# Linear attention, then an MLP: k and v loaded with nine tokens a partition and two heads side by side

## The chip, the cores and the metric

The kernel runs on one core of a Trainium2 chip. The metric is the time of one execution on the device in microseconds (us), less being better. The time before is the median of three runs. A profiled execution stands beside them; its span runs from the first to the last instruction. Engine names are those of the profile: PE is the matrix engine (PEld its weight loads), DVE the vector engine, ACT the scalar engine, POOL the general one, SP the queue that issues most transfers. PSUM is the memory that PE writes its sums into[...]; SBUF is the working memory of 128 partitions.

## The reference

There are 8 batches, 8 heads, 576 tokens (S) and 64 channels a head (D). The attention is linear, with cosine weights on the position; its output is the input x of a mixer with a low-rank token mix and a two-layer MLP.

```python
theta = np.pi / 2.0 * pos / S
phi(x) = concatenate([relu(x) * cos(theta), relu(x) * sin(theta)], axis=-1)   # 64 -> 128 features
q_p, k_p = phi(q), phi(k)
kv = einsum('bhsf,bhsd->bhfd', k_p, v)
z = sum(k_p, axis=2)
x = einsum('bhsf,bhfd->bhsd', q_p, kv) / (einsum('bhsf,bhf->bhs', q_p, z)[..., None] + 1e-6)
x -> [8, 576, 512]                       # heads side by side
u = x + (x^T @ U @ V)^T                  # U: 576x32, V: 32x576
out = u + relu(u @ w_ch1) @ w_ch2        # w_ch1: 512x2048, w_ch2: 2048x512
```

k's contraction runs over tokens. Which token lies on which partition, and in which order tokens are added, therefore does not matter for kv, as long as k and v agree; q's tokens decide where the rows of x stand.

## The kernel before, in words

**Layout.** A batch's 576 tokens are split into 512 and a tail of 64. Of the 512, partition p has tokens 4p to 4p+3, so each transfer (`load_main`, L75) has runs of four tokens, 1024 bytes, for each head and partition. The tail (`load_tail`, L81) has one token a partition on 64 partitions, runs of 256 bytes; even batches use partitions 0 to 63, odd ones 64 to 127 (`tail`). The staging tiles are `qst`, `kst`, `vst` for the main part and `qt`, `kt`, `vt` for the tail.

**Scaling.** `k_prep` and `q_prep` handle one chunk c at a time (0 to 3 are the four tokens of a partition, 4 is the tail): one instruction for the cosine half and one for the sine half, each on DVE (L230) or ACT (L228), over 8 heads x 64 channels. `cosw` and `sinw` hold the weight of each partition's token in a column for each chunk. The tail chunk goes into `k_tl` or `q_tl`, whose other 64 partitions were set to zero at the start. v is cast to `v_ext` (`v_prep`, `v_block`), with a column of ones after each head's 64, so that z comes out as column 65 of kv.

**kv.** `kv_unit` (L262) makes four heads: for each head five matmuls of 128 features x 65 columns, contracting 128 tokens each, accumulate in a PSUM tile; then one instruction casts the tile into `kv`. A batch takes two calls, 40 matmuls.

**After kv.** q is transposed, by PE (`qtr_unit`) for batches 0 to 2 and by DMA for the others. `x_unit` makes x for batches 2 to 7; for batches 0 and 1 the quicker chain `den_unit` (denominators, `rec`) and `xh_unit` does it. `A_unit` makes x^T U in 32-column tiles of PE, `u_unit` adds the low-rank part, and `g1_main`, `g1_tail` (g_ps, L491 and L511) and `g2_part` (o_ps, L543) are the two MLP layers, with ACT evicting `hid` (L500).

**Order.** The order of every engine's instructions is that of the program text. The main part is a list of slots, each one step of an MLP layer (four 512-column matmuls as a rule), for four pairs of batches. Between the slots, `PLAN` puts the attention of batches 2 to 7: for each batch a slot w at which kv is made, offsets for v, k, q and the loads, and the engines for each. Batches 0 and 1 are ordered by hand: batch 0's scalings and `chain0` come ahead of all slots, and batch 1's stand in `beside` and `chain1`, beside the first slots of batch 0. `keep_warm` issues matmuls on zeros, so that PE is not idle. PSUM tags stand for buffers: "X" two banks, "T" one, "g" three of one bank, "o" two of one bank.

**Loads at the start.** SP issues in the order: q half, q half, k half, k tail, q tail, v half's tail, v half, k half, v half's tail, v half (a half is four heads). A POOL instruction, `mark` (L738), reads a cell of batch 0's first v half; behind it in POOL's order stands the first load of w_ch1 (`w1_load`, L91), which therefore starts only when that half of v has landed.

Of the kernel before, what the change touches and what calls it, by code (L numbers as in the profile page):

```python
# [10 lines left out]
FP32 = mybir.dt.float32  # L11
# [6 lines left out]
def kernel(  # L18
# [28 lines left out]


    def tail(b):
        lo = TS * (b % 2)  # L50
        return slice(lo, lo + TS)
# [7 lines left out]

    kst, vst, qst, kt, vt, qt = {}, {}, {}, {}, {}, {}  # L60

    def alloc_k(b):
        kst[b] = pool.tile([P, H, 4, D], FP32, tag="kst", bufs=2, name="kst")
        kt[b] = pool.tile([P, H, D], FP32, tag="kt", bufs=2, name="kt")

    def alloc_v(b):
        vst[b] = pool.tile([P, H, 4, D], FP32, tag="vst", bufs=1, name="vst")
        vt[b] = pool.tile([P, H, D], FP32, tag="vt", bufs=1, name="vt")

# [41 lines left out]
    alloc_v(0)  # L111
    iota = const.tile([P, 5], FP32)
    nc.gpsimd.iota(
# [3 lines left out]
    for lo in (0, TS):  # L117
        nc.gpsimd.iota(
            out=iota[lo : lo + TS, 4:5], pattern=[[1, 1]], base=512, channel_multiplier=1,
            allow_small_or_imprecise_dtypes=True,  # L120
        )
    load_main(qst[0], q, 0, 0, 4)
    load_main(qst[0], q, 0, 4, 8)
    load_main(kst[0], k, 0, 0, 4)
    load_tail(kt[0], k, 0)
    load_tail(qt[0], q, 0)
    load_tail(vt[0], v, 0, 0, 4)
    load_main(vst[0], v, 0, 0, 4)
    load_main(kst[0], k, 0, 4, 8)
    load_tail(vt[0], v, 0, 4, 8)  # L130
    load_main(vst[0], v, 0, 4, 8)
    zero = const.tile([P, 512], BF16)
    V_.memset(zero, 0.0)
    halfpi = const.tile([P, 1], FP32)
    nc.vector.memset(halfpi, math.pi / 2.0)
    cosw = const.tile([P, 5], FP32)
    sinw = const.tile([P, 5], FP32)
    scale_ang = math.pi / (2.0 * S)
# [6 lines left out]

    k_tl = const.tile([P, H, 2 * D], BF16)
    v_ext = [const.tile([P, 5, H, E], BF16, name=f"v_ext{i}") for i in range(2)]
    q_tl = const.tile([P, H, 2 * D], BF16)
# [14 lines left out]
    for i in range(2):  # L163
        nc.gpsimd.dma_start(out=U_bf[tail(i), 4 + i, :], in_=moe_U[512:S, :])
    for g in range(4):
        V_.tensor_copy(out=four[:, g, :], in_=ident[0:R, 0:R])
    for i in range(2):
        V_.memset(v_ext[i][:, 4, :, :], 0.0)
        V_.memset(v_ext[i][:, 0:4, :, D:E], 1.0)
        V_.memset(v_ext[i][tail(i), 4, :, D:E], 1.0)  # L170
    V_.memset(k_tl, 0.0)
    V_.memset(q_tl, 0.0)
    V_.memset(q_tlT, 0.0)
    V_.memset(x_tl, 0.0)

    def keep_warm(n, tag, bufs):
# [30 lines left out]

    def v_prep(b, h0=0, h1=H, cs=range(5), engs=None):
        vx = v_ext[b % 2]
        for n, c in enumerate(cs):  # L210
            eng = engs[n] if engs else G_
            if eng is None:
                continue
            if c < 4:
                cast(eng, vx[:, c, h0:h1, 0:D], vst[b][:, h0:h1, c, :])
            else:
                cast(eng, vx[tail(b), 4, h0:h1, 0:D], vt[b][tail(b), h0:h1, :])

    def v_block(b, h0, h1, c0, c1, eng):
        cast(  # L220
            eng,
            v_ext[b % 2][:, c0:c1, h0:h1, 0:D].rearrange("p c h d -> p h c d"),
            vst[b][:, h0:h1, c0:c1, :],
        )

# [7 lines left out]

    def prep(dst, src, b, c, engs, h0, h1):
        rows = slice(0, P) if c < 4 else tail(b)
        for i, (w, eng) in enumerate(zip((cosw, sinw), engs)):
            if eng is not None:
                scaled_relu(
                    eng, dst[rows, h0:h1, i * D : i * D + D], src[rows], w[rows, c : c + 1]
                )  # L240

    def k_prep(b, c, engs, h0=0, h1=H):
        if b not in k_p:
            k_p[b] = pool.tile([P, 4, H, 2 * D], BF16, tag="k_p", bufs=1, name="k_p")
        src = kst[b][:, h0:h1, c, :] if c < 4 else kt[b][:, h0:h1, :]
        prep(k_p[b][:, c] if c < 4 else k_tl, src, b, c, engs, h0, h1)

    def q_prep(b, c, engs, h0=0, h1=H):
        if b not in q_p:
            q_p[b] = pool.tile([P, 4, H, 2 * D], BF16, tag="q_p", bufs=1, name="q_p")  # L250
        src = qst[b][:, h0:h1, c, :] if c < 4 else qt[b][:, h0:h1, :]
        prep(q_p[b][:, c] if c < 4 else q_tl, src, b, c, engs, h0, h1)

    def kv_unit(b, hg, tag, bufs, eng=None):
        if b not in kv_sb:
            kv_sb[b] = pool.tile([P, H, E], BF16, tag="kv", bufs=2, name="kv")
        acc = ps.tile([P, 4, E], FP32, tag=tag, bufs=bufs, name="kv_ps")
        vx = v_ext[b % 2]
        for i in range(4):
            h = hg * 4 + i  # L260
            for c in range(5):
                nc.tensor.matmul(  # L262
                    out=acc[:, i, :],
                    lhsT=k_p[b][:, c, h, :] if c < 4 else k_tl[:, h, :],
                    rhs=vx[:, c, h, :],
                    start=(c == 0),
                    stop=(c == 4),
                )
        cast(eng or V_, kv_sb[b][:, hg * 4 : hg * 4 + 4, :], acc)

# [298 lines left out]
    def loads(b, eng):  # L569
        def kk():  # L570
            alloc_k(b)
            load_tail(kt[b], k, b, eng=eng)
            load_main(kst[b], k, b, eng=eng)

        def vv():
            alloc_v(b)
            load_tail(vt[b], v, b, eng=eng)
            load_main(vst[b], v, b, eng=eng)

        def qq():  # L580
            alloc_q(b)
            load_tail(qt[b], q, b, eng=eng)
            load_main(qst[b], q, b, eng=eng)

        return kk, vv, qq
# [20 lines left out]
    def attention_plan(b):  # L606
# [4 lines left out]
        def put(at, f, *a, tag=False):  # L611
            if tag:
                a = a + spare(w + at)
            plan.append((w + at, lambda: f(b, *a)))

        for n, c in enumerate(ORD):
            put(v_at[0] + v_at[1] * n, v_prep, 0, H, (c,), (v_at[2],))
        for n, c in enumerate(ORD):
            put(k_at[0] + n, k_prep, c, VA if b == 3 and n > 1 else k_at[1])
            e0, e1 = q_at[1]  # L620
# [4 lines left out]
        if qtr is not None:  # L625
            for n, (c0, c1) in enumerate(((0, 2), (2, 4), (4, 5))):
                put(qtr + 2 * n, qtr_dma, c0, c1)
        put(0, kv_unit, 0, tag=True)
        put(2, kv_unit, 1, tag=True)
        for n, c in enumerate(ORD if qtr is None else range(5)):  # L630
# [25 lines left out]

    def chain0():
        v_prep(0, 0, 4, (4,), (A_,))
        v_block(0, 0, 4, 0, 3, V_)
        v_block(0, 0, 4, 3, 4, A_)  # L660
        qtr_unit(0, 4, 0, H, V_, *G3)
        keep_warm(2, "o", 2)
        for c in (0, 1):
            k_prep(0, c, (V_, A_), 4, 8)
        kv_unit(0, 0, "T", 1)
        keep_warm(2, "o", 2)
        for c in (2, 3):
            k_prep(0, c, (V_, A_), 4, 8)
        k_prep(0, 4, (A_, A_), 4, 8)
        rec0 = den_unit(0, 0, 4, "X", 1)  # L670
        v_prep(0, 4, 8, (4,), (G_,))
        v_block(0, 4, 8, 0, 4, G_)
        w1_load(1)
        for n, c in enumerate(TL):
            xh_unit(0, c, 0, 4, rec0, *(O2, O2, G3, G3, G3)[n], A_ if n == 1 else None)
        keep_warm(1, "X", 1)
        kv_unit(0, 1, "T", 1, A_)
        rec1 = den_unit(0, 4, 8, "X", 1)
# [13 lines left out]
    def chain1(fill):  # L692
        kv_unit(1, 0, "T", 1)
        fill(0)
        rec0 = den_unit(1, 0, 4, "X", 1)
        v_block(1, 4, 8, 0, 4, A_)
        fill(1)
        for n, c in enumerate(ORD):
            xh_unit(1, c, 0, 4, rec0, *O2)
            if n == 1:  # L700
                fill(2)
            if n == 3:
                kv_unit(1, 1, "T", 1, A_)
        fill(3)
# [27 lines left out]
    V_evac(V_)  # L732
    for c in TL:
        k_prep(0, c, (V_, A_ if c < 3 else V_), 0, 4)
    q_prep(0, 4, (V_, A_))
    keep_warm(10, "o", 2)

# [3 lines left out]
    alloc_q(1)  # L741
    load_main(qst[1], q, 1)
    load_tail(qt[1], q, 1)
    alloc_k(1)
    load_main(kst[1], k, 1)
    load_tail(kt[1], k, 1)
    alloc_v(1)
    load_tail(vt[1], v, 1)
    load_main(vst[1], v, 1, 0, 4)
    load_main(vst[1], v, 1, 4, 8)  # L750
    chain_end(0, a0)
# [14 lines left out]
    for n, c in enumerate(ORD):  # L766
# [3 lines left out]
        at(1 + n, lambda c=c, tg=tg: qtr_unit(1, c, eng=V_, tag=tg[0], bufs=tg[1]))  # L770
        at((4, 5, 5, 6, 6)[n], lambda c=c, n=n: k_prep(1, c, (V_, A_)))
    at(2, lambda: G_.tensor_copy(out=mark, in_=q_tlT[0:TS, 0, TS : TS + 1]))
    at(2, lambda: [w1_load(2), w1_load(3)])
    at(2, lambda: v_prep(1, 0, H, (4,), (G_,)))
    at(2, lambda: v_block(1, 0, 4, 0, 4, G_))
    at(6, lambda: [w2_load(n) for n in range(4)])
# [70 lines left out]
```

## Time and profile before

| | us |
|---|---|
| median of 3 runs (319.23 to 320.55) | 320.3 |
| profiled execution, its own time | 319.13 |
| its span | 317.4 |
| PE busy | 307.9 |
| DVE busy | 156.5 |
| ACT busy | 150.8 |
| POOL busy | 36.4 |

The engines' busy times overlap each other, so they don't add up to the span. PE's share is an average: PE is busy 19.15 of the first 24 us, part of that on zeros, 22.52 of the next 24, and nearly all the time after that. The granted clock of PE was full throughout. The loads of k and v are 1024 KB and 128 KB for a batch each: in the table of transfers `kst` takes a median of 7.9 us from issue to landing and `kt` 6.1.

### The profile page before, as it was taken

What the parts mean: (1) busy time and instruction counts of PE and PEld (TensorE: products, weight loads), DVE (VectorE), ACT (ScalarE), POOL (GpSimd) and SP (SyncE); (2) the same over time, 40 slices, a digit from 0 to 9 for tenths busy, and PEclk for the clock granted to TensorE, in tenths of its full rate; (3) what the DMA queues carried; (4) which work ended last, traced back from release to release, by engine and by line L of the source; (5) the groups of instructions that cost most, each with busy time, mean ns of one, the idle gap of its engine ahead of it and who ended that gap; (6) DMA issues with size and microseconds to landing.
All of it is one profiled execution on the core that took longest, in us unless ns stands there. A gap on an engine that the chain in (4) does not pass through costs nothing.

```text
span 317.4 us, 5790 instructions
## 1 busy us (share of the span) xinstructions
PE 307.9 (97%) x2378; PEld 161.6 (51%) x2378; DVE 156.5 (49%) x355; ACT 150.8 (48%) x260; POOL 36.4 (11%) x67
## 2 busy tenths in 40 slices
PE   6889899999999999999999999999999999999996
PEld 2566554475545444475455444574454444464443
DVE  7879653843877554037826584254736510001211
ACT  5749655686806256659300187559300166650000
POOL 4324301200121220000121100000121100000000
PEclk9999999999999999999999999999999999999999
DMA  7999999964386928860999569900691130001122
GB/s 225 314 267 269 205 232 331 323 185 168 94 189 166 300 67 188 253 206 2 206 256 294 192 131 232 327 9 33 158 191 68 66 83 0 2 0 68 66 89 77
DMA packets 83803, 51.82 MB, mean 163 GB/s; under 512 B 52066, under 2 KB 81026, under 8 KB 83778
## 3 DMA queue, kind: packets, MB, share of 16 engines
q1 hardware_dynamic: 76850, 40.05, 47.3%
q0 software_dynamic: 6784, 11.35, 15.0%
q8 instruction: 18, 0.29, 0.4%
q10 hardware_dynamic: 144, 0.07, 0.1%
q14 instruction: 7, 0.06, 0.1%
HBM read 36.86 MB, written 9.44 MB: 146 GB/s over the span
## 4 chain that ended last, share of the span: by engine, by line
PE 87%; DMA 5%; ACT 4%; SPq 1%; DVE 1%; POOL 0%; issue 0%; DVEq 0%
PE o_ps L543 39%; PE g_ps L491 33%; PE gt_ps L511 4%; DMA w_bf<-in_moe_w_ch_dram 3%; PE kv_ps L262 3%; PE va_ps L407 3%; PE x_ps L363 3%; DMA vst<-in_v_dram 2%; ACT hid L500 2%; PE a_ps L390 1%; PE t_ps L279 1%; ACT k_p L228 1%; ACT q_p L228 1%; SPq L81 1%; SPq L75 0%; POOL mark L738 0%
## 5 line engine op out<-in xcount | busy, mean ns | idle before, releaser
L500 ACT ACTIVATE hid<-g_ps 128x512 bf16<-128x512 f32 x128 | 76.2, 596 | 100.8 <-PE g_ps L491 100.4
L543 PE MATMUL o_ps<-w_bf,hid 128*128 128x512 bf16 (+2 forms) x528 | 119.2, 373 | 0.0
L491 PE MATMUL g_ps<-uT,w_bf 128*128 128x512 bf16 x512 | 118.5, 379 | 0.1
L491 PEld LDWEIGHTS <-w_bf 128*128 128x128 bf16 x512 | 48.8, 98 | 56.0 <-issue 0.4
L543 PEld LDWEIGHTS <-hid 128*128 128x128 bf16 x528 | 48.7, 98 | 52.8 <-issue 1.7
L553 DVE TENSOR_TENSOR o_sb<-u_bf,o_ps 128x512 f32<-128x512 bf16 (+2 forms) x33 | 22.1, 668 | 62.7 <-PE o_ps L543 62.6
L563 POOL DMA_DIRECT2D out_dram<-o_sb x24 | 13.5, 561 | 165.0 <-DVE o_sb L553 155.0
L408 DVE TENSOR_TENSOR u_bf<-x_bf,va_ps 128x512 bf16<-128x512 bf16 x32 | 21.7, 685 | 10.2 <-PE va_ps L407 10.1
L105 DVE CAST kv<-kv_ps 128x260 bf16<-128x260 f32 x14 | 6.0, 428 | 31.6 <-PE kv_ps L262 31.6
L373 DVE TENSOR_TENSOR x_bf<-x_ps,rec 128x512 bf16<-128x512 f32 x24 | 16.6, 691 | 0.8
L228 ACT ACTIVATE q_p<-qst,sinw 128x512 bf16<-128x512 f32 (+1 forms) x24 | 15.1, 658 | 2.2 <-DMA qst<-in_q_dram 2.2
L511 PE MATMUL gt_ps<-uT_tl,w_bf 128*128 128x128 bf16 x256 | 15.6, 219 | 0.0
L407 PE MATMUL va_ps<-A_sb,V_bf 128*128 128x512 bf16 x40 | 15.2, 379 | 0.0
L543 PE MATMUL o_ps<-w_bf,hid_tl 128*128 128x512 bf16 x64 | 15.1, 379 | 0.0
L230 DVE TENSOR_SCALAR k_p<-kst,cosw 128x512 bf16<-128x512 f32 (+1 forms) x31 | 14.9, 503 | 0.0
L313 DVE TENSOR_SCALAR rec<-x_ps 128x8 f32<-128x8 f32 (+1 forms) x30 | 4.9, 165 | 20.2 <-PE x_ps L363 20.2
L511 PEld LDWEIGHTS <-w_bf 128*128 128x128 bf16 x256 | 14.6, 98 | 0.5
L262 PEld LDWEIGHTS <-k_p 128*128 128x128 bf16 x256 | 11.4, 97 | 4.8 <-ACT k_p L228 1.2
L262 PE MATMUL kv_ps<-v_ext,k_p 128*128 128x65 bf16 x256 | 12.2, 193 | 0.9 <-ACT k_p L228 0.9
L518 ACT ACTIVATE hid_tl<-gt_ps 128x512 bf16<-128x512 f32 x16 | 9.4, 597 | 5.5 <-PE gt_ps L511 5.5
L363 PEld LDWEIGHTS <-q_pT 128*128 128x128 bf16 x192 | 9.1, 98 | 5.5 <-issue 0.6
L230 DVE TENSOR_SCALAR q_p<-qst,cosw 128x512 bf16<-128x512 f32 (+1 forms) x28 | 11.6, 435 | 0.1
(106 smaller groups left out, 253.1 us busy)
## 6 DMA issues: line engine op xcount, KB each, us to landing
qst<-in_q_dram SPq DMA_DIRECT2D x7, 1024.0 KB, 8.9
kst<-in_k_dram SPq DMA_DIRECT2D x7, 1024.0 KB, 7.9
vst<-in_v_dram SPq DMA_DIRECT2D x6, 1024.0 KB, 8.2
out_dram<-o_sb POOLq DMA_DIRECT2D x24, 256.0 KB, 3.6
w_bf<-in_moe_w_ch_dram POOLq DMA_DIRECT2D x8, 512.0 KB, 9.3
vst<-in_v_dram SPq DMA_DIRECT2D x4, 512.0 KB, 7.9
out_dram<-o_sb SPq DMA_DIRECT2D x7, 256.0 KB, 2.4
qst<-in_q_dram SPq DMA_DIRECT2D x2, 512.0 KB, 3.8
```

The source lines that it names most:

```text
L228: nc.scalar.activation(out=o, in_=i, func=AF.Relu, bias=0.0, scale=w)
L230: eng.tensor_scalar(out=o, in0=i, scalar1=0.0, scalar2=w, op0=ALU.max, op1=ALU.mult)
L262: nc.tensor.matmul(out=acc[:, i, :], lhsT=k_p[b][:, c, h, :] if c < 4 else k_tl[:, h, :], rhs=vx[:, c, h, :], start=(c == 0), stop=(c == 4),)
L363: nc.tensor.matmul(out=acc[:, g, i * E : i * E + E], lhsT=qT_of(b, c, h), rhs=kv_sb[b][:, h, :], start=True, stop=True,)
L373: nc.vector.tensor_tensor(out=x_of(b, c, rows).rearrange("p (g i d) -> p g i d", g=2, d=D), in0=view[:, :, :, 0:D], in1=rec[rows].unsqueez ...
L407: nc.tensor.matmul(out=va, lhsT=V_bf[:, c, :], rhs=A_sb[b], start=True, stop=True)
L408: nc.vector.tensor_tensor(out=u_bf[b][:, c, :] if c < 4 else u_tl[b // 2][rows, :], in0=x_of(b, c, rows), in1=va[rows, :], op=ALU.add,)
L491: nc.tensor.matmul(out=g_ps.rearrange("p (c t) -> p c t", c=4), lhsT=w1_bf[:, d, j * P : j * P + P], rhs=uT[b][:, :, d, :], start=(d == 0) ...
L500: nc.scalar.activation(out=hid[b][:, j, :], in_=g_ps, func=AF.Relu, bias=0.0, scale=1.0)
L511: nc.tensor.matmul(out=g_ps[:, jj, :], lhsT=w1_bf[:, d, j * P : j * P + P], rhs=uT_tl[pr][:, d, :], start=(d == 0), stop=(d == 3),)
L543: nc.tensor.matmul(out=o[:, cols], lhsT=lhs[:, j, c * P : c * P + P], rhs=w2_bf[:, j, cols], start=(j == 0), stop=(j == NJ - 1),)
L553: nc.vector.tensor_tensor(out=o_sb[:, cols], in0=u[:, cols], in1=o[:, cols], op=ALU.add)
```

## The change

k and v of a batch are laid out anew. Partition p of the lower half (0 to 63) has tokens 9p to 9p+8 of the even head of a pair, and partition 64+p the same tokens of the odd head. All 576 tokens fit, so k and v have no tail; a run is nine tokens, 2304 bytes, and one transfer (`load_nine`) brings all four head pairs, or two of them. q stays as it was.

- `k_prep` has nine chunks instead of five, each of 4 pairs x 64 = 256 elements on 128 partitions instead of 512. The weights for them are columns 5 to 13 of `cosw` and `sinw`.
- `v_prep` casts one head pair at a time (9 x 64 elements), four instructions a batch; `v_block` is gone.
- `kv_unit` contracts 64 tokens a matmul: for each pair and chunk one matmul on the lower 64 partitions into one PSUM bank and one on the upper 64 into another, 72 a batch instead of 40. Batches 2 to 7 make it in one call with one cast at w+1; batches 0 and 1 in two calls. The tile has the tag X of two banks.
- `k_tl` and the zeroing of v's tails are gone; the `four` copies come after the other settings of constants.
- Batch 0's loads go q half, q half, k half, v half, q tail, k half, v half, and its scalings and `chain0` are ordered anew, with POOL taking part of k's second half. `den_unit` of the first half takes T instead of X. Batch 1's k comes before its q tail, and its scalings run three chunks a slot in slots 4 to 6.

```diff
+    def load_nine(dst, src, b, g0=0, g1=4, eng=None):
+        (eng or nc.sync).dma_start(
+            out=dst[:, g0:g1, :, :].rearrange("p g c d -> p g (c d)"),
+            in_=src[b].rearrange("(g hh) (p c) d -> (hh p) g (c d)", hh=2, c=9)[:, g0:g1, :],
+        )
...
-    load_main(kst[0], k, 0, 0, 4)
-    load_tail(kt[0], k, 0)
+    load_nine(kst[0], k, 0, 0, 2)
+    load_nine(vst[0], v, 0, 0, 2)
     load_tail(qt[0], q, 0)
-    load_tail(vt[0], v, 0, 0, 4)
-    load_main(vst[0], v, 0, 0, 4)
-    load_main(kst[0], k, 0, 4, 8)
-    load_tail(vt[0], v, 0, 4, 8)
-    load_main(vst[0], v, 0, 4, 8)
+    load_nine(kst[0], k, 0, 2, 4)
+    load_nine(vst[0], v, 0, 2, 4)
...
     for i in range(2):
-        V_.memset(v_ext[i][:, 4, :, :], 0.0)
-        V_.memset(v_ext[i][:, 0:4, :, D:E], 1.0)
-        V_.memset(v_ext[i][tail(i), 4, :, D:E], 1.0)
-    V_.memset(k_tl, 0.0)
+        V_.memset(v_ext[i][:, :, :, D:E], 1.0)
...
+    def v_prep(b, g, eng):
+        cast(eng, v_ext[b % 2][:, g, :, 0:D], vst[b][:, g, :, :])
...
+    def k_prep(b, c, engs, g0=0, g1=4):
+        if b not in k_p:
+            k_p[b] = pool.tile([P, 9, 4, 2 * D], BF16, tag="k_p", bufs=1, name="k_p")
+        for i, (w, eng) in enumerate(zip((cosw, sinw), engs)):
+            if eng is not None:
+                scaled_relu(
+                    eng, k_p[b][:, c, g0:g1, i * D : i * D + D], kst[b][:, g0:g1, c, :],
+                    w[:, 5 + c : 6 + c],
+                )
...
+    def kv_unit(b, g0=0, g1=4, eng=None):
...
+        acc = ps.tile([P, 2, 512], FP32, tag="X", bufs=1, name="kv_ps")
+        for g in range(g0, g1):
+            for c in range(9):
+                for hh in range(2):
+                    rows = slice(hh * TS, hh * TS + TS)
+                    nc.tensor.matmul(
+                        out=acc[:, hh, (g - g0) * E : (g - g0) * E + E],
+                        lhsT=k_p[b][rows, c, g, :],
+                        rhs=v_ext[b % 2][rows, g, c, :],
+                        start=(c == 0),
+                        stop=(c == 8),
+                    )
...
+        for g in range(4):
+            put(v_at[0] + v_at[1] * g, v_prep, g, v_at[2])
+        for c in range(9):
+            put(k_at[0] + c * 5 // 9, k_prep, c, VA if b == 3 and c > 3 else k_at[1])
...
-        put(0, kv_unit, 0, tag=True)
-        put(2, kv_unit, 1, tag=True)
+        put(1, kv_unit)
...
     def chain0():
-        v_prep(0, 0, 4, (4,), (A_,))
-        v_block(0, 0, 4, 0, 3, V_)
-        v_block(0, 0, 4, 3, 4, A_)
-        qtr_unit(0, 4, 0, H, V_, *G3)
-        keep_warm(2, "o", 2)
-        for c in (0, 1):
-            k_prep(0, c, (V_, A_), 4, 8)
-        kv_unit(0, 0, "T", 1)
-        keep_warm(2, "o", 2)
-        for c in (2, 3):
-            k_prep(0, c, (V_, A_), 4, 8)
-        k_prep(0, 4, (A_, A_), 4, 8)
-        rec0 = den_unit(0, 0, 4, "X", 1)
-        v_prep(0, 4, 8, (4,), (G_,))
-        v_block(0, 4, 8, 0, 4, G_)
+        v_prep(0, 0, V_)
+        v_prep(0, 1, A_)
+        q_prep(0, 4, (V_, A_))
+        kv_unit(0, 0, 2)
+        keep_warm(2, "o", 2)
+        qtr_unit(0, 4, 0, H, V_, *G3)
+        for c in range(9):
+            k_prep(0, c, (V_ if c < 4 else G_, A_), 2, 4)
+        rec0 = den_unit(0, 0, 4, "T", 1)
+        for g in (2, 3):
+            v_prep(0, g, G_)
         w1_load(1)
...
-        keep_warm(1, "X", 1)
-        kv_unit(0, 1, "T", 1, A_)
+        keep_warm(2, "T", 1)
+        kv_unit(0, 2, 4, A_)
...
-    for c in TL:
-        k_prep(0, c, (V_, A_ if c < 3 else V_), 0, 4)
-    q_prep(0, 4, (V_, A_))
-    keep_warm(10, "o", 2)
+    for c in range(9):
+        k_prep(0, c, (V_, V_ if c in (4, 8) else A_), 0, 2)
+    keep_warm(11, "o", 2)
...
-        at((4, 5, 5, 6, 6)[n], lambda c=c, n=n: k_prep(1, c, (V_, A_)))
+    for c in range(9):
+        at(4 + c // 3, lambda c=c: k_prep(1, c, (V_, A_)))
```

## The prediction

> **What bounds the kernel now.** I read the page first, then a table of busy time over stretches of the span, then the chain of waits, then the timeline of single engines. The page names the engine, and the table says where it is the limit (columns: stretch, its length, then busy us and instruction count of PE, PE's weight loads, DVE, ACT, POOL, then granted clock, DMA share, GB/s):
>
> ```profile
> PE 307.9 (97%) x2378; PEld 161.6 (51%) x2378; DVE 156.5 (49%) x355; ACT 150.8 (48%) x260; POOL 36.4 (11%) x67
> ...
> 0.00:24.00 24.00, 19.15 (x227) 11.13 (x228) 18.51 (x60) 14.01 (x32) 7.53 (x18) 1.00 1.02 268
> 24.00:48.00 24.00, 22.52 (x254) 13.54 (x253) 17.09 (x37) 16.90 (x30) 6.52 (x9) 1.00 1.20 238
> 48.00:284.00 236.00, 235.93 (x1745) 122.45 (x1744) 114.60 (x249) 119.92 (x200) 22.38 (x40) 1.00 0.59 158
> ```
>
> From 48 us on PE is busy 235.93 of 236 us and the table of waits shows no wait of PE there: a matmul added or taken away there counts in full, and DVE, ACT, POOL and DMA have cover. Before 48 us PE waits[...]. So the change has a front stage, a stage of batch 1, and a PE stage for batches 2 to 7.
>
> The chain of waits up to 48 us (start, us, what) names what ended last:
>
> ```profile
> 4.79 7.81 DMA vst<-in_v_dram
> ...
> 12.65 1.20 POOL mark L738
> 13.85 9.01 DMA w_bf<-in_moe_w_ch_dram
> ...
> 31.19 1.33 ACT k_p L228 x2
> ...
> 33.01 1.23 ACT k_p L228 x2
> ...
> 34.29 0.70 PE kv_ps L262 x17
> ```
>
> It says that batch 0's first half of v starts the first weights' load, which ends at 22.86 us, just when the first g_ps matmuls start (22.91), and that later ACT's k_p holds PE's kv matmuls (PE idle 0.9 us in all). But the first link has a twin: batch 0's attention ends at the same moment, and it is led by DVE, which is busy 18.51 of 24 us. DVE's timeline:
>
> ```profile
> 5.55 0.27 DVE L174 MEMSET x_tl<- 128x256 uint32 x1
> 5.74 1.01 DVE L230 TENSOR_SCALAR q_p<-qst,cosw 128x256 bf16<-128x256 f32 x4
> ...
> 15.56 1.41 DVE L230 TENSOR_SCALAR k_p<-kst,cosw 128x256 bf16<-128x256 f32 x2
> 16.89 0.16 DVE L313 TENSOR_SCALAR rec<-d_ps 128x20 f32<-128x20 f32 x1
> ```
>
> q's first half landed at 4.54 (issued 0.74, 3.80 to landing), yet DVE starts on it at 5.74, behind memsets; the reciprocal that opens batch 0's x waits until 16.89 for k_p scalings in front of it on DVE. A faster load alone therefore moves the first g_ps matmul little.
>
> [...] The trace has no 64-row tile, but it has 32-column tiles in a_ps[...]:
>
> ```profile
> 87.88 1.89 PE L543 MATMUL o_ps<-w_bf,hid_tl 128*128 128x512 bf16 x8
> 89.70 0.40 PE L390 MATMUL a_ps<-x_bf,U_bf 128*32 128x512 bf16 x4
> 89.92 0.38 PE L390 MATMUL a_ps<-x_tl,U_bf 128*32 128x512 bf16 x1
> 90.23 1.04 PE L543 MATMUL o_ps<-w_bf,hid_tl 128*128 128x512 bf16 x4
> ```
>
> Four matmuls of 512 columns take 0.40 us together, one takes 0.38. Eight o_ps at 0.216 each (1.73 us in the chain) end their issue at 89.61, a_ps starts at 89.70; the fifth would free PE at 89.92 + 0.22 = 90.14, PE goes on at 90.23. A switch costs 0.09 each way, 0.18 for in and out. [...] here DVE's scaling takes 476 ns for 512 elements and 346 for 256, ACT's 710 and 497. [...] above, two scalings of 0.35 take 1.41 us while POOL casts v_ext from 15.70 to 16.82.
>
> **The change, part by part.** The sum is made against the profiled execution: span 317.4, its own time 319.13 (1.7 around the span). The median shown, 320.3, is 1.2 above it, and I add that at the end.
>
> *kv matmuls, batches 2 to 7.* Before, one half-batch of 20 matmuls goes from 74.91 to 75.51 and the next from 77.24 to 77.84: 0.60 us, 30 ns each, 1.20 a batch. After, 72 in 36 pairs. If the two halves run together, a pair costs one 30 ns step plus the issue of the second pair member; I take 35 ns: 1.26. With one switch in and out 1.44, so +0.24 a batch, +1.4 for six, all on PE's path. Bounds: 30 ns a pair and no switch, 1.08, gives -0.12 a batch (-0.7); if a half's matmul cannot start until the other's is through, each costs 25 ns (the 16 one-column d_ps matmuls at 35.49 take 0.54, less 0.16 for the last: 25 ns a step) to 30 ns, 1.80 to 2.16 a batch, with the switch +0.78 to +1.14, or +4.7 to +6.8 for six.
>
> *kv matmuls, batches 0 and 1.* Four calls of 18 pairs, 0.63 + 0.18 against 0.60: +0.2 each, +0.8; all four lie on chains that lead on. Bounds -0.2 and +2.0 (36 at 30 ns and the switch, +0.66 each, less what idle PE absorbs).
>
> *Front.* Memsets of k_tl and the v_ext tails go (0.48, 2 x 0.65), two small ones come (about 0.1 each), the `four` copies (0.4) move behind the others: DVE is free well before q lands, so q_p starts at about 4.6, 1.1 earlier. Then k_p of half 0 on DVE is 11 instructions of 128 elements instead of 7 of 256. Start to start, 256 elements take 0.26 (1.01 for four) and 512 take 0.40, so 128 take about 0.20: 2.2 against 1.8, +0.4. ACT has 7 at about 0.29 (0.40 for 256, 0.61 for 512) against 3 at 0.40, +0.8, covered by DVE. v's casts are 0.45 on DVE against 0.55. kv is issued ahead of the tail's transposes, which saves DVE's wait for them (0.32). Half 1 then asks DVE for 4 small scalings instead of 4 larger, 0.8 against 2.4 with the blocked ones; ACT for 9 at 0.29, 2.6, against 6 at 0.40. POOL gets 5 scalings that the trace does not show there; its 64x256 cast takes 0.40, so I take 0.35 each, 1.8, plus two casts of about 0.65. They fall on 11 to 15 us, where DVE works through k_p[...]. Gain without clashes 1.2, with all of them about 0: I take -0.7, bounds -1.6 and +0.8.
>
> *Loads.* Before, v's first half needs q, k's half and three tails first and lands at 12.59; now 2.23 MB stand up to it instead of 2.37, and no tails. At 300 and 343 GB/s (2 to 6 us, large runs only) against 252 and 235 (6 to 10, tails among them) it should land near 9.5. So w1's load starts 3 us earlier, and waits for nobody; POOL's mark and load issues move with it, ahead of POOL's scalings. SP has fewer issues (0.6 to 0.9 each). I cost all of this at nothing, because DVE's chain is then last by 2 to 3 us; if DVE were not in the way, up to -3.
>
> *Batch 1.* ACT's sin half of k is 9 instructions of 256 at 0.40, 3.6, against 0.70 and 4 at 0.61, 3.1: +0.5, and ACT is the chain there, with hid's evictions queued between. DVE's 9 at 0.26 are shorter than before. Bounds 0 and +1.
>
> *Batches 2 to 7, other engines.* k on two engine-slots is 18 instructions of 256 instead of 10 of 512: 4.7 against 4.0 on DVE, 7.2 against 6.1 on ACT, a batch; the engines are half busy (114.60 and 119.92 of 236), and a lead of 5 slots or more (0.9 us each; batch 3 has the least) hides it. Cost 0; without cover, a late kv or hid eviction of 1 us in some batches, +2 in all. kv's eviction becomes one of 520 elements, about 0.69 against two of 0.43. The accumulator now holds X, which x needs three slots later.
>
> Sum: 1.4 + 0.8 - 0.7 + 0.5 = +2.0. The profiled execution would take 321.1, the median 320.3 + 2.0 = 322.3. About 0.5% (1.6 us) is what a measurement here tells from no change, so I forecast **slower, by 0.6%**.
>
> **Rivals.** *Not slower: the front pays for PE.* Mechanism: DVE's early start and the unblocked reciprocal, place 4.6 to 17 us, price the full -1.2, with pairs at 30 ns: 8 x (1.08 + 0.18 - 1.20) = +0.5, and two more switches +0.4, ACT +0.5. That is +0.2, 320.5. It decides once the first o or g step of the main part comes over 1 us earlier than 22.9. For it: q's 1.2 us idle in SBUF. [...] Chance 0.30. *Faster:* the same, and the load link was the true bound, so that up to 3 us come: +0.2 - 2.5, 318.0. For it: the chain as printed; against it: DVE's 18.51 of 24. Chance 0.12. *The halves do not overlap*, so the change does not do what the row split is for: +4.7 to +6.8 in six batches, about +1.5 in the first two, front -0.7, ACT +0.5: 326.3 to 328.4. For it: a 25 ns floor per matmul even at one column; against it: a_ps. Chance 0.26. The forecast itself has 0.32.
>
> **From this the numbers.** Faster 0.12, same 0.30, slower 0.32 + 0.26 = 0.58. The forecast case by itself spans 321.9 to 324. Low 318.6 keeps most of the faster case, high 328.2 most of the last one.
>
> **What would show it.** Steps are right if kv_ps takes 1.2 to 1.4 us a batch with a gap of about 0.09 on either side, if q_p starts on DVE at 4.6, rec falls at 16 to 16.5, the first g_ps at about 22.2, and ACT's last k_p of batch 1 lies 0.5 later than the first g_ps would put it. kv_ps at 1.8 or more means no overlap; rec at 17 or later, with DVE scalings of 1 us beside POOL's, means that the front gave nothing; first g_ps before 21 means that loads, not DVE, led. PE idle after 48 us would prove wrong that the smaller scalings are hidden.

## The result, and the profile after

The changed kernel is slower: 324.12 us median (323.45 to 325.0) against 320.43 of the kernel before on the same chip, ratio 1.012, 95% interval 1.0079 to 1.0161. Its profiled execution took 323.96 with a span of 322.1, so the span grew by 4.7 from 317.4. The sum in the prediction was +2.0; the loss is about twice that.

The answering lines of the page and of the table of stretches (same columns as before):

```profile
PE 312.9 (97%) x2634; PEld 163.2 (51%) x2634; DVE 157.0 (49%) x386; ACT 152.2 (47%) x281; POOL 39.2 (12%) x72
...
0.00:24.00 24.00, 20.34 (x248) 11.70 (x249) 15.95 (x57) 15.11 (x37) 10.24 (x25) 0.93 0.99 285
24.00:48.00 24.00, 21.88 (x273) 13.27 (x271) 16.84 (x40) 15.31 (x31) 6.11 (x9) 1.00 1.03 189
48.00:290.00 242.00, 241.88 (x1968) 124.42 (x1968) 117.82 (x279) 121.78 (x214) 22.89 (x38) 1.00 0.62 157
```

Four things are to be seen. From 48 us on PE is full again, so the smaller scalings of DVE and ACT stayed hidden. DVE has less to do in the first 24 us (15.95 against 18.51), POOL more (10.24 against 7.53). PE waits more in the second stretch (busy 21.88 us against 22.52). And PE's granted clock averaged 0.93 in the first, which the kernel before did not show.

The chain of waits up to 48 us has a new link that nothing of before answers to:

```profile
3.67 9.36 DMA kst<-in_k_dram
...
13.93 13.23 DMA qt<-in_q_dram
27.19 0.49 DVE q_tl L219
...
29.45 0.30 POOL mark L761
...
32.16 1.29 ACT k_p L217 x3
...
35.61 1.20 ACT k_p L217 x3
36.87 0.51 PE kv_ps L254 x20
```

The first `mark` (L738 before) and the transfer of w_bf behind it are no longer in it. Batch 1's q tail is: issued at 13.93, landed at 27.16. In the kernel before it was issued at 13.47 and landed 6.5 us later, at 20.0 (its tile `qt`, 13 to 14 us):

```profile
L81 SPq DMA_DIRECT2D qt<-in_q_dram x1: 607/607/607, 13.5 to 13.5; - x1
...
DMA to landing us min/median/max: 6.5/6.5/6.5
```

On SP's queue k (1152 KB) of batch 1 now stands ahead of it, issued at 7.88 and landed at 24.73; SP also waits with the tail until DVE has read batch 0's (3.5 us), since `qt` has one buffer. Behind the tail the chain runs over its scaling and its transposes to a second `mark` (L761), a POOL instruction that reads the transposed tail and holds back two loads of w_bf and the casts of v; then come ACT's nine sine scalings, with `hid` evictions between them.

DVE's timeline, for the lines at 5.74 and 16.89 before:

```profile
4.63 1.14 DVE L219 TENSOR_SCALAR q_p<-qst,cosw 128x256 bf16<-128x256 f32 x4 [1.55 <-DMA qst<-in_q_dram]
...
16.50 0.17 DVE L309 TENSOR_SCALAR rec<-d_ps 128x20 f32<-128x20 f32 x1
```

and PE's, one batch of kv between two o_ps steps:

```profile
77.34 1.89 PE L539 MATMUL o_ps<-w_bf,hid 128*128 128x512 bf16 x8
79.16 1.33 PE L254 MATMUL kv_ps<-v_ext,k_p 64*128 64x65 bf16 x72
80.43 1.90 PE L539 MATMUL o_ps<-w_bf,hid 128*128 128x512 bf16 x8
```

Eight o_ps at 0.216 are issued by 79.07, and o_ps goes on at 80.43: a batch of kv takes 1.36, against 1.20 before, with both switches in it (the 0.09 that the prediction reads on either side of a_ps).

**Where the time went.** The same instructions' start can be compared between traces. Four marks serve for every run below: the first g_ps matmul of all, the first d_ps of batch 1, the g_ps matmul that before starts at 47.9, and the last g_ps matmul. Each number is the start less that of before, in us.

| kernel | first g_ps | d_ps, batch 1 | g_ps at 47.9 | last g_ps |
|---|---|---|---|---|
| changed | +1.43 | +2.39 | +3.29 | +4.47 |
| changed, again | -0.12 | +2.82 | +3.46 | +4.63 |
| q tail ahead of k | +0.27 | +1.22 | +1.43 | +2.60 |
| mended (below) | -0.07 | +0.19 | +1.10 | +2.27 |
| halves apart | +0.94 | +2.68 | +3.12 | +6.61 |
| before, k ahead of q tail | +0.56 | +3.31 | +3.32 | +3.31 |
| before, early DVE start | -0.05 | -0.05 | +1.55 | +1.55 |

In the second profile of the changed kernel batch 1 takes most of the loss (from -0.12 to +3.46); in the first it shares it with the front. The main part takes 1.17 or 1.18 in each of the first four rows (4.47 less 3.29 in the first).

### The profile page after: what moved, and what is told of

Same layout as the page of the kernel before. It is cut to its first block, busy times and chain, and to the rows that moved or that the text cites. A ratio compares the mean times of both kernels' runs of the same rounds, so it can differ in the third digit from the quotient of the medians.

```text
span 322.1 us, 6341 instructions
## 1 busy us (share of the span) xinstructions
PE 312.9 (97%) x2634; PEld 163.2 (51%) x2634; DVE 157.0 (49%) x386; ACT 152.2 (47%) x281; POOL 39.2 (12%) x72
## 3 DMA queue, kind: packets, MB, share of 16 engines
q1 hardware_dynamic: 60194, 40.05, 47.9%
## 4 chain that ended last, share of the span: by engine, by line
PE 85%; DMA 7%; ACT 4%; DVE 1%; SPq 1%; POOL 1%; issue 1%; DVEq 0%; POOLq 0%
PE o_ps L539 39%; PE g_ps L487 31%; DMA qt<-in_q_dram 4%; PE gt_ps L507 4%; DMA kst<-in_k_dram 3%; PE kv_ps L254 3%; PE va_ps L403 3%; PE x_ps L359 2%; ACT k_p L217 1%; ACT hid L496 1%; PE a_ps L386 1%; ACT q_p L217 1%; PE t_ps L275 1%; POOL w_bf L97 0%; DVE q_p L219 0%
## 5 line engine op out<-in xcount | busy, mean ns | idle before, releaser
L559 POOL DMA_DIRECT2D out_dram<-o_sb x24 | 14.7, 612 | 166.0 <-DVE o_sb L549 156.6
L404 DVE TENSOR_TENSOR u_bf<-x_bf,va_ps 128x512 bf16<-128x512 bf16 x32 | 21.7, 683 | 10.6 <-PE va_ps L403 10.6
L219 DVE TENSOR_SCALAR k_p<-kst,cosw 128x256 bf16<-128x256 f32 (+1 forms) x63 | 19.8, 340 | 0.0
L111 DVE CAST kv<-kv_ps 128x520 bf16<-128x520 f32 (+1 forms) x8 | 5.1, 632 | 28.8 <-PE kv_ps L254 28.8
L217 ACT ACTIVATE k_p<-kst,sinw 128x256 bf16<-128x256 f32 (+1 forms) x43 | 17.2, 455 | 0.1
L254 PE MATMUL kv_ps<-v_ext,k_p 64*128 64x65 bf16 x576 | 12.0, 191 | 2.0 <-ACT k_p L217 1.4
L254 PEld LDWEIGHTS <-k_p 64*128 64x128 bf16 x576 | 10.7, 94 | 6.2 <-issue 3.4
L219 DVE TENSOR_SCALAR q_p<-qst,cosw 128x512 bf16<-128x512 f32 (+1 forms) x28 | 12.3, 459 | 1.6 <-DMA qst<-in_q_dram 1.6
L219 DVE TENSOR_SCALAR k_p<-kst,sinw 128x256 bf16<-128x256 f32 (+1 forms) x38 | 13.0, 342 | 0.0
```

The lines of the kernel that those rows point to most:

```text
L217: nc.scalar.activation(out=o, in_=i, func=AF.Relu, bias=0.0, scale=w)
L219: eng.tensor_scalar(out=o, in0=i, scalar1=0.0, scalar2=w, op0=ALU.max, op1=ALU.mult)
L254: nc.tensor.matmul(out=acc[:, hh, (g - g0) * E : (g - g0) * E + E], lhsT=k_p[b][rows, c, g, :], rhs=v_ext[b % 2][rows, g, c, :], start=(c ...
L404: nc.vector.tensor_tensor(out=u_bf[b][:, c, :] if c < 4 else u_tl[b // 2][rows, :], in0=x_of(b, c, rows), in1=va[rows, :], op=ALU.add,)
L559: eng.dma_start(out=out[b, 0:512, cols].rearrange("(p c) n -> p c n", c=4)[:, c, :], in_=o_sb[:, cols],)
```

## The experiments

The theory after the comparison: the loss is batch 1, where q's tail is stuck on SP's queue, plus ACT's scalings there, plus the kv matmuls. Rivals: PE's half clock in the front; POOL's scalings; kv halves that don't overlap. In each timed execution the mean granted clock of PE is recorded, and some kernels show executions with 0.995 or less where others mostly show 1.0; these are called below full clock here.

**The changed kernel once more, unaltered.**

> The changed kernel itself, unaltered, on the same chip as the three that follow, to compare them with. From its first trace: 4.7 us more span than before, of which about 1.4 stood at the first g_ps matmul, 2.5 at the first d_ps of batch 1, 3.3 at 50 us and 4.5 at the end. Expected here: 1.008 to 1.016 of the time before. If the low granted clock at 20 to 23.5 us in that trace was chance, this trace may lack it, and then the first g_ps should come near 23.3 instead of 24.3.

323.94 us, ratio 1.0122 (1.0084 to 1.0161). The clock was full throughout this profile, and the first g_ps came at the time of before, 1.55 earlier than in the first profile. Yet at batch 1's d_ps it was 0.43 later. The table of waits from 22 to 48 us shows why (who waited, for whom: us in total, times, longest):

```profile
DVE q_tl L219 <- DMA qt<-in_q_dram: 3.3, 1, 3.3
...
PE t_ps L275 <- ACT q_tl L217: 2.9, 1, 2.9
```

What the front gains or loses ends in the wait for q's tail. The half clock of the first profile is therefore not the cause of the 1.2%: the two executions of this kernel at full clock took 323.8 and 324.1, and nine of before at full clock have a median of 319.9.

**q's tail ahead of k, in the changed kernel.**

```diff
 load_main(qst[1], q, 1)
+load_tail(qt[1], q, 1)
 alloc_k(1)
 load_nine(kst[1], k, 1)
-load_tail(qt[1], q, 1)
```

> Queue theory: batch 1's q tail landed at 27.16 because 1152 KB of k stood ahead of it in SP's queue, and DVE and ACT waited 1.3 us for it. With the tail issued ahead of k the wait goes: DVE starts q_tl right after its uT cast, near 26, and the time falls by about 1.3 us (2.5 at most), to 1.006 to 1.010 of before. Rival, the clock and POOL in batch 0's chain: it is they that hold batch 1, and moving the tail gives less than 0.4 us.

In the trace the wait is gone. DVE's timeline has the scaling without a wait ahead of it, 2.4 us earlier:

```profile
24.75 0.48 DVE L219 TENSOR_SCALAR q_tl<-qt,cosw 64x512 bf16<-64x512 f32 x1
```

d_ps of batch 1 starts 1.60 earlier than in the changed kernel's second profile (2.82 less 1.22), and the last g_ps 2.03. What comes next is no longer the tail. PE waits for the second transfer of w_bf, which lands at 29.39 (table of waits, 22 to 48 us):

```profile
PE g_ps L487 <- DMA w_bf<-in_moe_w_ch_dram: 0.9, 1, 0.9
```

The median did not follow: 323.82, ratio 1.0111 (1.0072 to 1.015). Of seven executions two had a full mean clock (322.1 and 323.8), the other five 0.982 to 0.995 (322.8 to 325.3). The trace supports the queue; the times alone do not.

**The same part alone, put into the kernel before.**

```diff
 load_main(qst[1], q, 1)
-load_tail(qt[1], q, 1)
 alloc_k(1)
 load_main(kst[1], k, 1)
 load_tail(kt[1], k, 1)
+load_tail(qt[1], q, 1)
```

> The kernel before with one part of the change alone: batch 1's k (main part and its tail) issued ahead of q's tail on SP's queue. Queue theory (q's tail lands behind whatever stands in front of it on the queue, and DVE's and ACT's scaling of it, then PE's transposes, wait): q's tail lands 5 to 8 us later than its 20.0, at 25 to 28, PE waits 1.5 to 3 us for t_ps, median +1.5 to +2.5. Rival (q's tail is late only since the changed kernel's loads run slower as a whole, or since PE's clock is lower there): it lands within 2 us of 20.0 and the median moves by less than 0.7.

323.56 against 320.13, ratio 1.0125 (1.0078 to 1.0173): this one move costs as much as the whole change, with no other part of it present. Its table of waits, 14 to 48 us:

```profile
POOL mark L772 <- DVE q_tlT L105: 13.4, 1, 13.4
...
DVE q_tl L230 <- DMA qt<-in_q_dram: 3.0, 1, 3.0
...
PE t_ps L279 <- ACT q_tl L228: 2.6, 1, 2.6
```

q's tail lands at 28.0 instead of 20.0. PE's wait is 2.6 us, and POOL's second `mark`, which reads the transposed tail, holds up the casts of v behind it (9.2 us of waiting before). The loss of +3.31 is there at batch 1's d_ps and stays constant to the end. It is larger than the 2.0 that the opposite move takes out of the changed kernel's trace: there the wait for w_bf comes next, and here 0.56 of the loss lies at the first g_ps already, whose w_bf landed at 23.42 instead of 22.86.

**More matmuls on zeros ahead of batch 0's second denominators, in the changed kernel.**

```diff
 kv_unit(0, 2, 4, A_)
+keep_warm(2, "T", 1)
```

> Two more matmuls on zeros while PE waits for the cast of batch 0's second kv (it idled 0.48 us there). Clock theory: PE's idle spots at 17 to 19 us let the granted clock fall to half from about 20.3 to 23.5 us, which cost about 1.0 us; with them filled the clock stays full and the time falls by about 1 us, to 1.008 of before. Queue theory: the clock is beside the point, since batch 1 waits for its q tail until 27.2 us anyway, and the time stays within 0.3 us of the unaltered changed kernel.

324.89, ratio 1.0147 (1.0104 to 1.0189). The first g_ps came at +0.64, then the wait for q's tail took over (DVE waits 2.9 us for it, PE 2.5), and the half clock appeared at another place, about 30 to 33 us. The clock theory's number failed: filling that gap gains nothing.

**The kv halves one after the other instead of in turn.**

```diff
 for g in range(g0, g1):
-    for c in range(9):
-        for hh in range(2):
+    for hh in range(2):
+        for c in range(9):
```

> The nine chunks of one half of the partitions all before the nine of the other half, so that neighbours in PE's order share their half[...]. If overlap of the halves is what holds kv at 1.36 us a batch with its switches (a pair each 33 ns in the trace), a batch goes to 72 x 30 ns + 0.18 = 2.3 us, 1.0 more, and the time rises by 6 to 8 us, to 1.031 to 1.037 of before. If matmuls of 64 rows are short by themselves, without overlap, the time doesn't change.

326.96, ratio 1.0218 (1.0177 to 1.0258). The timeline of PE for the same batch:

```profile
77.17 1.89 PE L539 MATMUL o_ps<-w_bf,hid 128*128 128x512 bf16 x8
78.99 1.72 PE L254 MATMUL kv_ps<-v_ext,k_p 64*128 64x65 bf16 x72
80.64 2.76 PE L539 MATMUL o_ps<-w_bf,hid 128*128 128x512 bf16 x12
```

From 77.17 + 1.73 = 78.90 to 80.64 it is 1.74 us, against 1.36 in the changed kernel: 0.38 a batch, or 2.3 for six, which is what the marks show (3.49 against 1.18 between the third and the fourth). So the two halves do overlap in the changed kernel: in its trace the matmuls start in pairs 3 to 4 ns apart, and less the 0.18 for the switches a pair takes 32.8 ns.

The expectation of 1.0 a batch was not met, because this order does not take the overlap away. The starts in the trace read as rows of nine with steps of 32 to 38 ns (0, 38, 73, 106, 138, 171, 203, 237 and 269 ns for the first row), and each row begins about 180 ns after the one before it, while that one still runs. The mean of 21.7 ns over the 72 matmuls is therefore not the price of one. A half alone takes about 33 ns a matmul; with no overlap at all a batch would take some 2.55 us with its switches (an estimate: 72 x 33 ns and 0.18), 1.2 more than in turn.

**The front's early DVE start alone, in the kernel before.** The constants of batch 1's `v_ext`, of `q_tlT` and of `x_tl` are set later; `v_const(i)` stands for the three memsets of `v_ext[i]`, and `v_const(1)` follows batch 0's first x units.

```diff
-    for i in range(2):
-        V_.memset(v_ext[i][:, 4, :, :], 0.0)
...
+    v_const(0)
-    V_.memset(q_tlT, 0.0)
-    V_.memset(x_tl, 0.0)
...
+    V_.memset(q_tlT, 0.0)
+    V_.memset(x_tl, 0.0)
     V_four("X", 1)
```

> The kernel before with DVE's constants for later use (v_ext of batch 1, q_tlT, x_tl) set after the q scalings in place of ahead of them, so that DVE starts on q when it lands, 1.1 us earlier. If DVE's chain sets the first g_ps matmul, as the prediction put it: first g_ps 0.7 to 1.2 earlier than 22.9, median -0.5 to -1.2. If the loads and w1's transfer set it: rec is early by up to 1 us, first g_ps within 0.3 of 22.9 behind a wait for w_bf, median within 0.4.

320.49 against 320.13, ratio 0.9998 (0.9979 to 1.0017). rec fell at 15.79 instead of 16.89, and then PE waited, as its timeline shows:

```profile
22.86 0.60 PE L491 MATMUL g_ps<-uT,w_bf 128*128 128x512 bf16 x2 [0.85 <-DMA w_bf<-in_moe_w_ch_dram]
```

The first g_ps stands at 22.86 against 22.91. Both chains, DVE's and w1's, end at the same moment before; taking DVE's away gains nothing. (The +1.55 at the third mark is half clock between 36 and 39 us in this profile.)

**The load part of the front on top of it**: the first half of v ahead of the tails.

```diff
+    load_main(vst[0], v, 0, 0, 4)
     load_tail(kt[0], k, 0)
-    load_tail(qt[0], q, 0)
     load_tail(vt[0], v, 0, 0, 4)
-    load_main(vst[0], v, 0, 0, 4)
+    load_tail(qt[0], q, 0)
```

> The same with batch 0's first half of v issued ahead of the tails of k, v and q, the load part of the change without its layout. If both DVE and the transfer of w1 (which starts on that half's arrival) set the first g_ps together, this one gains where the early DVE start alone did not: mark 1 to 2 us earlier than 12.65, first g_ps 1 to 2 earlier than 22.9, median -1 to -2 against before. If DVE alone set it, no better than the early start alone. If the tails, now later, are last on DVE (k_tl, q_tl), rec comes later and the median is 0 to +0.5.

320.73, ratio 1.002 (1.0 to 1.0039). `mark` came only 0.56 earlier than at 12.65, and the tails came too late: k_tl waits on DVE until 12.64, and PE 2.6 us for q's tail. (PE's clock was at half from 14.24 to 17.66 in this profile, so the stages after that are not read; the five executions at full clock have a median of 319.9, as before has.) Without the layout that removes the tails, this load order gains nothing.

**ACT's relief in batch 1**, in the changed kernel with q's tail ahead of k: three of nine sine scalings on DVE.

```diff
-        at(4 + c // 3, lambda c=c: k_prep(1, c, (V_, A_)))
+        at(4 + c // 3, lambda c=c: k_prep(1, c, (V_, V_ if c % 3 == 2 else A_)))
```

> The changed kernel with batch 1's q tail ahead of k, and with three of the nine sin scalings of batch 1's k on DVE in place of ACT. If ACT's nine instructions are the chain of batch 1 once q's tail is in time (prediction: +0.5): d_ps of batch 1 0.5 to 1.2 earlier than with q's tail ahead alone, profiled span about 319.5, median 0.5 to 1 lower than 323.8. If PE itself (more and longer kv matmuls) or the clock holds what is left: within 0.3 of it.

323.22, ratio 1.0099 (1.0065 to 1.0132): 0.6 below the run without it, which the intervals do not separate. In the trace the first g_ps was at +2.06 after half clock in the front, and d_ps of batch 1 at +2.31. Between those marks it loses 0.25, where the kernel without the relief lost 0.95. But 0.86 of that 0.95 was PE's wait for w_bf, which is absent here because the front is later, so it says nothing of ACT. The stretch that holds ACT's scalings runs from the 17th g_ps matmul to batch 1's d_ps, 28.14 to 35.49 before. PE's timeline in the kernel before, in the changed kernel and here:

```profile
28.14 1.03 PE L491 MATMUL g_ps<-uT,w_bf 128*128 128x512 bf16 x4
...
30.60 1.03 PE L487 MATMUL g_ps<-uT,w_bf 128*128 128x512 bf16 x4
...
37.88 0.54 PE L317 MATMUL d_ps<-kv,q_pT 128*128 128x1 bf16 x16 [0.20 <-DVE kv L111]
...
30.19 1.03 PE L487 MATMUL g_ps<-uT,w_bf 128*128 128x512 bf16 x4
...
37.81 0.56 PE L317 MATMUL d_ps<-kv,q_pT 128*128 128x1 bf16 x16 [0.20 <-DVE kv L111]
```

That is 7.35 us before, 7.28 in the changed kernel and 7.62 here; it is 7.28 in the changed kernel's second profile and 7.29 with q's tail ahead. ACT's nine scalings cost batch 1 nothing, and the relief makes it 0.3 longer.

**Mended**: the same, with five more matmuls on zeros in the wait for v (`keep_warm(16, "o", 2)` for 11) and only two of batch 0's k scalings on POOL:

```diff
-            k_prep(0, c, (V_ if c < 4 else G_, A_), 2, 4)
+            k_prep(0, c, (V_ if c < 7 else G_, A_), 2, 4)
```

> The changed kernel with batch 1's q tail ahead of k, ACT's relief, three of POOL's five k scalings of batch 0 on DVE, and five more matmuls[...]. If the queue, ACT and POOL's 0.72 us scalings are what the front and batch 1 lose, only the kv matmuls are left: about +1.0 for batches 2 to 7 and +0.4 for 0 and 1, profiled span at full clock 318.5 to 319.5, median 321 to 322. If PE's idle stretches and the clock keep the loss: median 323 or more as before the mending.

The profile has full clock and the row of the table above: front -0.07, d_ps of batch 1 +0.19, last g_ps +2.27, span 319.7. PE no longer waits for w_bf: POOL comes to that load 2.7 us sooner (15.49), and it lands at 27.40 instead of 29.39. The +0.19 is the relief, which makes the stretch from the 17th g_ps to d_ps 7.62 us here too. Between the second and the third mark 0.56 of the 0.91 is one gap that the profile puts to "issue", which is in some of the profiles and not in others:

```profile
41.21 0.25 PE L317 MATMUL d_ps<-kv,q_pT 128*128 128x1 bf16 x4 [0.56 <-issue]
```

The median is 323.18, ratio 1.0096 (1.0059 to 1.0133), because seven of nine executions had a mean clock of 0.982 to 0.995; the two with full clock took 321.7 and 321.8, against a median of 319.8 for the 30 of 44 of before with full clock. So the span met the first theory's words nearly, and the median met the rival's.

**The relief in the kernel before, with the early start.**

```diff
-        at((4, 5, 5, 6, 6)[n], lambda c=c, n=n: k_prep(1, c, (V_, A_)))
+        at((4, 5, 5, 6, 6)[n], lambda c=c, n=n: k_prep(1, c, (V_, V_ if n in (2, 4) else A_)))
```

> The kernel before with the early DVE start, and with two of the five sin scalings of batch 1's k on DVE in place of ACT. If ACT's scalings of k hold batch 1's kv (PE idle 0.9 us for them in the trace of before), PE's d_ps of batch 1 comes 0.7 to 1.2 earlier after the first g_ps than before, median -0.5 to -1.0 against before. If DVE takes over as the bound there (it is half busy, but copies q_pT in the same stretch), within 0.3 of before.

321.41 against 319.99, ratio 1.0044 (1.002 to 1.0068), slower. The timeline of PE names the new wait:

```profile
33.87 0.19 PE L262 MATMUL kv_ps<-v_ext,k_p 128*128 128x65 bf16 x1 [0.87 <-DVE k_p L230]
34.70 0.20 PE L262 MATMUL kv_ps<-v_ext,k_p 128*128 128x65 bf16 x1 [0.64 <-DVE k_p L230]
```

Moved work of 512 elements on DVE, between the copies of q_pT, is later there than on ACT: DVE takes over as the bound, the second outcome named. From the first g_ps to batch 1's d_ps the trace loses 0.64. The rest of the median goes with the clock: 15 of 20 executions were below full clock, and the five at full clock have a median of 320.1, against 319.8 for the 30 of before.

**The first weights' load released by k's half instead of v's**, on top of that.

```diff
-    G_.tensor_copy(out=mark, in_=vst[0][0:TS, 0, 0, 0:1])
+    G_.tensor_copy(out=mark, in_=kst[0][0:TS, 0, 0, 0:1])
```

> The same with the first weights' load released by the first half of k in place of v's, the one part of the change's front that was not tried: w1 starts earlier. If the early DVE start gains nothing only because w1 lands at 22.8 all the same, first g_ps now comes 0.7 to 1.0 earlier (about 22.0) and the median is 0.7 to 1.0 below the run with the early start and ACT's relief. If w1's transfer and v's share one limited bandwidth, v's halves land 1 to 2 us later, rec and kv with them, and nothing or less than nothing is left (0 to +1).

Ratio 1.0032 (1.0 to 1.0063) over 12 of 22 executions, no gain; nine of the others had a mean clock of 0.984 or less, and one took 830 us. The profiled execution had PE at half clock from 19.23 to 29.48 us, and the lowest mean clock of all (0.979), so its stage times are not read. The three executions at full clock took 319.2 to 319.6, below the 320.1 of the run above at full clock; they are too few to tell, and whether w1's earlier release gains anything stays open.

**More matmuls on zeros in the kernel before.**

```diff
-    keep_warm(12, "X", 1)
+    keep_warm(17, "X", 1)
...
-    keep_warm(10, "o", 2)
+    keep_warm(14, "o", 2)
...
-    at(7, lambda: keep_warm(2, "X", 1))
+    at(7, lambda: keep_warm(6, "X", 1))
```

> The kernel before with 5, 4 and 4 more matmuls of zeros in three stretches in which PE waits (for q, for q's tail, for batch 1's k), 0.22 us each, so that they fill the wait and end before it does. Theory: PE's clock falls to half for about 3 us after such stretches, by chance, and each fall costs about 1.6 us; then fewer executions have a mean clock below 1 than the 24 of 44 of before in the last comparison, and the median is 0.5 to 1.2 below before, at an unchanged span at full clock (317.5). Rival: the falls have nothing to do with these waits; share and median stay within 0.3. If the fillers push real work back, span at full clock and median rise by up to 1.

The count of before in that text is wrong: 14 of 44 executions were below full clock, not 24. In this comparison it was 5 of 19 for before and none of 14 here (the lowest is 0.998). That speaks for the fillers, in few executions. But the median was 319.64 against 319.26, ratio 1.0002 (0.9978 to 1.0027): no gain. In the trace the first g_ps is 0.81 late behind a 0.9 us wait for w_bf, and the executions at full clock have a median of 319.6 against 319.2, so what the clock gives is lost there. Neither theory holds as written, and no version here beats the kernel before.

## Why the prediction was right, and where it was mis-sized

**Direction and main stage: right.** kv of batches 2 to 7 was to cost +1.4. It costs 0.16 a batch (1.36 against 1.20), about 1.0 of the 1.17 that the main part loses. The pair takes 32.8 ns where 35 was taken. What a_ps had shown holds here for the 64-row halves: the two run side by side (32.8 ns a pair, where a half alone takes about 33 a matmul), and a switch costs 0.09 each way. kv_ps starts at 79.16 after an issue that ends at 79.07; o_ps goes on at 80.43, 0.13 after the last pair's start at 80.30, and a pair takes 0.03 of that. Ahead of the 128-row kv_ps of before there is no such gap: o_ps at 75.51, with 1.73 of issue, and kv_ps at 77.24. But a pair's 32.8 ns is no better than the 30 ns of a whole 128-row matmul, so splitting the rows buys PE nothing: 36 pairs take 1.18 us where 40 whole matmuls took 1.20, and what a batch loses is the 0.18 of the two switches.

**The rival without overlap was priced too low.** It took 25 to 30 ns for each matmul from one-column d_ps. A half alone takes about 33, so no overlap would have been about +8 for six batches (an estimate: 2.55 against 1.20 each) and not +4.7 to +6.8. The run with the halves one after the other does not measure this, since they still overlap in part there.

**"SP has fewer issues ... I cost all of this at nothing" is the step that failed.** It looked at batch 0's loads only. The same diff moves batch 1's q tail behind k on SP. In the runs the tail took 13.23 us from issue to landing behind k's 1152 KB, and 6.5 ahead of k. In the changed kernel's second profile, at full clock, PE comes to the tail's transposes 5.61 us after the first g_ps, against 2.60 before: 3.0 us. Taking the wait out gains 1.6 at batch 1's d_ps and 2.0 at the end, since the wait for w_bf is next. Alone in the kernel before, the move costs 3.3.

**Front, -0.7: about -0.1.** q_p did start at 4.63 and rec fell at 16.50, as foretold. But that DVE alone leads was wrong for the kernel before: the early start alone moved the first g_ps by 0.05, since w1 lands at the same time. In the changed kernel v's half landed at 10.79, not near 9.5 (the 2.23 and 2.37 MB in that sum are in two units; in KB it is 2176 against 2368). `mark` came at 10.84 instead of 12.65, and w1's transfer took 10.9 us instead of 9.0 in the first profile. In the second it landed at 20.81, two us ahead of the first g_ps (22.79), so batch 0's attention alone is last there. It gained little: POOL's scalings were taken at 0.35 each and take 0.72, so its casts of v end at 18.08 and the second kv waits for them. POOL's timeline in the first profile:

```profile
13.22 3.62 POOL L219 TENSOR_SCALAR k_p<-kst,cosw 128x128 bf16<-128x128 f32 x5 [1.34 <-DMA kst<-in_k_dram]
16.80 1.28 POOL L111 CAST v_ext<-vst 128x576 bf16<-128x576 f32 x2
```

In the mended kernel, with three of these on DVE, POOL's casts end at 15.54, but rec falls at 16.91 and the first g_ps gains only 0.07. The clashes of DVE and POOL that the sum allowed for did not show: DVE's four k_p between 15.67 and 16.58, beside POOL's, took 0.28 to 0.32 each (0.27 to 0.45 in the second profile), and its nine cosine ones of 10.43 to 12.55, ahead of POOL's, 0.27 to 0.37.

**Batch 1's ACT, +0.5: nothing.** From the 17th g_ps to batch 1's d_ps it takes 7.28 us against 7.35 before. The scalings themselves were priced rightly (0.40 apart, 1.20 for three in the chain), and ACT's last one ends 0.12 later against that g_ps than before (6.21 us behind it, against 6.09). But behind it 0.51 us of kv is left in the chain, where before it was 0.70. The +0.5 left that out.

**Hidden scalings, 0: right but for one step.** PE is busy 241.88 of 242 us from 48 us on. One o_ps step, at 230.61, takes 0.42 us instead of 0.22 in both profiles of the changed kernel and not before; an eviction of o_ps that stands behind four k scalings on DVE ends just then (230.98), which may be the reason.

The changed kernel's +4.63 in its second profile is thus -0.1 for the front, +3.0 for q's tail, -0.1 for the stretch with ACT's scalings, +0.6 from there to the third mark (0.3 of it a gap that the profile puts to "issue") and +1.2 for the main part. Of these the sum had only the main part near its size. The mended kernel, at full clock, loses 2.27 in the trace and 2.0 in two timed executions, close to the +2.0 of the sum, but by luck: the front's gain, ACT's +0.5 and the +0.8 for kv in batches 0 and 1 all came out near nothing at batch 1's d_ps (+0.19, with the relief's 0.3 in it), while 0.56 of the mended loss is the unexplained gap.

## What to carry to other kernels

When a diff reorders loads, write out the whole issue order of each queue, for the later batches too: here a 128 KB transfer behind a 1152 KB one of the same queue landed 2.4 us after that one (27.16, 24.73), and the single-buffered tile made the issuing queue itself wait (3.5 us). Ask of a bound which other chain ends at the same moment before you count a gain; here two did, and taking one away gave nothing. When a wait is taken out, look for the wait that comes next before you credit what is left to an engine: here it was a transfer of w_bf, and not the scalings on ACT. Splitting rows to run matmuls side by side pays only if the pairs, with their switches, take less than the whole matmuls they replace: here it was 1.36 us for 36 pairs against 1.20 for 40 whole ones.

## What the runs showed of the hardware that was not expected

PE's granted clock falls to half for 3.4 us at a time (20.48 to 23.90 in the changed kernel's first profile, 36.46 to 39.88 in that of the early DVE start; once 10.2 us, 19.23 to 29.48 with w1 released by k's half), in some executions of the same kernel and not in others. In the table of stretches of the changed kernel's first profile it shows as clock in the third column from the right:

```profile
20.00:22.00 2.00, 2.00 (x24) 1.45 (x24) 1.33 (x4) 0.38 (x1) 0.00 (x0) 0.62 1.07 375
22.00:24.00 2.00, 2.00 (x18) 0.76 (x17) 0.75 (x2) 1.08 (x2) 0.00 (x0) 0.53 1.20 254
```

One such fall lowers the mean clock by 0.005 and goes with 1.1 to 1.7 us (of before, in three comparisons: 319.88 to 321.0, 319.95 to 321.3, 319.78 to 321.49). PE's waits don't tell when one comes. With v ahead of the tails PE did nothing from 12 to 14 us and the fall began at 14.24; but in the changed kernel's first profile it followed waits of no more than 1.4 us (12.1 to 13.55), and that of the early DVE start no wait over 0.85 us in the 14 us before it, while the second profile of the changed kernel, with PE idle for 2.85 us at a stretch (to 28.40), kept its clock. What sets it off in one execution and not in the next stays open, and with it why the repaired kernels, with 5 of 7, 6 of 8 and 7 of 9 executions below full clock against 14 of 44 of before, give so little of their shorter span to the median.
